# A longer look ahead before TensorE turns back from 64x64 parts, with new order and engine strings, in a fused attention and FFT-gate kernel

## The chip, the cores and the metric

One core of one Trainium2 chip. The metric is the device time of one execution in microseconds (us); lower is better. Times of the kernel before: median 951.72 us of 3 runs (948.12 to 954.63).

## The reference

For each of 8 batches, with S = 3136 rows, a model width of 256 and a key width of 64, all in float32:

```python
scores = scale * np.matmul(z, z.transpose(0, 2, 1))      # scale = 1 / S
attn = np.maximum(scores, 0.0) ** 2
x = u * np.matmul(attn, v)                               # [8, 3136, 256]

proj = x @ w_proj                                        # 256 -> 768
x1, x2, x3 = (proj[..., :D].copy(), proj[..., D:2 * D].copy(), proj[..., 2 * D:].copy())
X2 = np.fft.rfft(x2, n=S, axis=1)
H = np.fft.rfft(filter_fft, n=S, axis=0)[None, :, :]
x2_conv = np.fft.irfft(X2 * H, n=S, axis=1)
y = x1 * x2_conv * x3
return (y @ w_out).astype(np.float32)
```

The first half is attention with a squared ReLU in place of softmax, gated by u; the second a gate with a long circular convolution, done by FFT.

## The kernel before

**Tiles.** The 3136 rows of a batch are 64 x 49. They are handled as 25 tiles of 128 rows (the last has 64), and as 7 chunks of columns, `CHUNKS` = 512 five times, then 256 and 320. The matmuls are in bf16 and sum in PSUM, which is used as 4 pairs of banks (`ps_s`, 128 x 1024 float32 each). The transforms are products with matrices of sines and cosines, in two stages: the first (`dft1`, L998) over the 64, by full tables T1; the second (`forward` and `inverse`, issued by `quads`, L1100) over the 49, with tables S2 and TZ.

**Units of TensorE work.** All of TensorE's work is cut into 2637 units, each a short run of matmuls, all issued through `matmul` (L515, so all show as L516):

- S (512 units): scores of a pair of tiles for one chunk, `score_mm` (L1729), reading `zT_t`. The result is emptied from PSUM by a ReLU into R (L1919 on ACT, L1921 on DVE) and squared into A (L1928 on ACT, L1930 on DVE). The score matrix is symmetric, so part of A is also transposed by DMA into mirror tiles (`M_t`, `M2e_t`, `M2o_t`) and used for other chunks.
- w and v (648 each): the two halves of weighing v by one pair of tiles, `weigh` (L1772), reading `A_t` or a mirror tile and `v_t`. The two halves of the array's rows sum in two banks of a pair, and the halves swap banks between w and v.
- A (424): the projections (`xT_t`, `wp`) and the first stage of the transform (`x_t`, `T`). B (229) and Z (40): the filter's transform at the start, the last stage of the inverse transform (`conv_in_t`, `T`) and the output product (`wo`, `yT_t`); Z holds the late ones of the last batches.
- Q (136): the second stage of the transform, forward (`spec_in_t`, S2) and inverse (`xh`, TZ). Between the two, DVE multiplies by the filter's spectrum (L1357, L1361, L1362). Its tables are 49 or 64 rows by 64 columns.

**Forms of the array.** A Q unit runs in 64x64 parts of the array: four matmuls at a time, one for each half of the rows and of the output partitions. Any other unit runs by default in parts of 64 rows by all 128 columns, two at a time. It can also run in 64x64 parts: `parts_of` (L570) then gives two halves of the output partitions in place of one whole, and each matmul is issued as two. A few transposes at the start use the whole array. In the profile the forms are told by their shape: `64*128` or `64*64`, rows by columns.

**What sets the order.** The program is laid out ahead of time by a planner (`Plan`, `go` at L336), which walks through a string `ORDER`, one letter for a unit of TensorE; the next unit in TensorE's program is the one that the letter names. S, w and v are taken strictly in turn; A, B and Z from the first 6 of their queue and Q from the first 4, the one ready earliest. A second string, `ENGINES`, holds one letter for each of 1426 jobs that either ACT or DVE can do (the ReLU and the square, and the copies out of PSUM): a or d. The planner's own clock, with costs per operation, sets the order of the jobs on each engine. DMA queues run from SP and POOL; POOL casts u, v and z on their way in.

The form of a unit follows from the string alone:

```python
            form = "F" if task.full else "Q" if k == "Q" else "H"
            if form == "H" and self.form == "Q" and "Q" in ORDER[self.at + 1 : self.at + 1 + NEAR]:
                form = "Q"
            if self.form is not None and self.form != form:
                start += FORM
            self.form = form
```

So once a Q unit has turned the array to 64x64 parts, the units behind it stay in them as long as one of the next `NEAR` letters is a Q; otherwise they turn back. `FORM` = 0.16 us is what the planner books for a turn. `NEAR` is 6 (L44).

Of the kernel before, what the change touches and what calls it, by code (L numbers as in the profile page):

```python
# [48 lines left out]


ORDER = (
    "ASSAwSSSwvBAAvSSwSwwSvSvwvwSvvSwSvwSvSwSvwwSvwvvSwwwSwSwSvAvAwwvSSvvwAvSvSwwABvSvwvBvSwwAvwSAwSvwASA"
    "vvAvwSAwAwSvSAvAvwSAvwSwwSvAvASwwwwvvwvBBvwvSSvvwSSwBvBwvSvwSSwAvwvSvwwwAASvAwwBvBwvSwSAvvAvwSSvSwwA"
    "BASBvvwwSvwvvvSwwwSwvvSAvAvwSAvwwSAvvwAvSwwwASvvSvAwSvSwABwSBvwwSSwvwASvSvwAwvvASAvvwwSvvSASAwAwASvS"
    "wSvwBABvwAvSSwSvvwSSvwSvwwBSBvvwSwwwSvvSwAwAvSAvwAAwSvASvvAQQvAwSwwQQvAwAASvSAvAvwAwSwSwAwSAAwwASvwS"
    "vvQvvQSwvQvASvQwAwASwSAvwvASvwAvAvAwSSwwQSvAwASQvvAwQvvSAvwQSwAvwQwAwAQvASvvQvwSwwSQvAwwvSQwAvwSvQSw"
    "wSvvQwAwSAvwSwvvSvvvvSAwAwwSvvQSwAvwQSAvvSwwQASvAwwQvwvvSwQwAvASvSvwSSwAwAwSvSvvvSAwAvAwASvwSwAvAvSw"
    "wwASvSAvwvASSAvwBSwBAvvASwwSwABAwSvBBwBAwASvSvSvAwvAwvSwSwwABAABAvSvvSvSAwABvBAwAwwwSSvSvvBSvBBvwSBw"
    "AvwAwAvAvSwwwvSBSBwSvvSvAwSwABvBwAvASwSwvSAvBABSvvwwSvSwwSvAvvQAwQwwwQSwvvwQBwvQBvwQvBAvSBAvvSwAvAww"
    "ASvASvSwwwSSSwvwvwvSSvQvwQAwAQvwBwBQvvSvQvAwwwwQASvvwvBSwwvBvSwvSSvSwAvSvAQASAwQwwSSvwASAwAvSAwvQvAQ"  # L60
    "AvSvwSwwwwSSAvvAvvSwvSwwvSvSwwvASAwSvwSwvBAvBASvwSwwBSAvBAvwBSBSvwBvBAvSvAwwwwSSAvvAvSSwSwvAvABABAAv"
    "AwSwBwASBvAvBwBSvBwBwAAAvAvvSwwAvSSAvwwwSAvAvSwSvSwAwASvwvSBvBAwSAvvSwQSvwAvBQBAwwSwQwSwQvSvQwvvwQvA"
    "wAAQwAwSwBvSvSvBwvSvQvSvAwAQvBwBQwSQwwwSvwQQwSwvBvSBvAvSAvvvSAwAwSAvAwvSwvvAQAwSwwwSvvvSvSAwwSASvvBS"
    "wBSwAvASvwwwQSQvwwvvASSAvwvwSAvASwvSvwwASwAwSvvvSvAwAwSwwASAvSvBwvSwwBAvABvBvASwwASwAvABSvBSwvwvSBvS"
    "BAvAwwSwASwABvwBSAvAvSwwSwBvBABvBwwAvASwvSABvBBvABvASvwSvAwwSwASwAvSAvvSAwSAvwwSSAvAwwSQvwwQSvSvBvBA"
    "SvwABvBwvAwAQvwSvSQvwwQwSwwwAQvvvAvBQvBSwQBwwBSvSvvSAvAAwwSAvQwAQwAvwSwSAvvAwSvSvQvwQSwwBvSQvBwvSwQv"
    "vwwwSAvwSwwvvSvAvSQvwQASvwAvSwSvwASwAAwSwwSAwASASvvwwSvASwvSvAAvAwSvvAvAvwSvwSvwSvwwSBwSBwBvBSwwSvBB"
    "BBSvwwSAvAAvvSSAwvwvwSASvvvwwSAvSvAwBwBSAwwwSSwSvvAvABABAwvwASAAwASvvSwwSvSvwvvSvvSwSwAvSwvSAvSwwwBS"
    "vSwBwSvwvBBBBvSwvvwAvvwSwAAvSvwAAAwAwSAvSvAvSwAQvSwQwBvSQwwBAvAQvwvQwvAwAwQSvwSwQvBwQvwwSBvQvvSAwwQA"
    "vQvBwwSSvBvvwSwvvSwvwAASvAAwSwvQAvSwSAwwvSSvvvwQSwSvwQvwSQvSwvASAAwAwSwwQAvvSAvwvASwvAASwASvvvwwSvBS"  # L70
    "vwBwSSvvSwSAwABvBwSvSwAwBvAABvAwSwASvAAvASSwvBvBwwSwwSSvAwAvAvASwvSSvvBwBAvSwwAASwAwBAvABBvBwvSvSAvw"
    "ABvBBAwBwSAwwBSvBvSSvwwASvSAwAvAAwSvAvwSAvASvBwBAwAvSwvAwAQwwSwQSvvvSQvBvSBwwABwwSAvvBwSvQSwSwvBQvvv"
    "BQwwASAvQvQwSwwwQSvvSwQvAwvAQSvwwSvQvBwQBwSvwSwvSvAvwwAwvASAvwwSvSvQASAvvAQwSAvwSAvwASvwwwSAwAQvvSwS"
    "wSvSvwAvwvABvSwwBvSSvwAvAvwSwwSAvAAvvSAwSwSvASwABwBwBSvBwSvvSvwSwBvBSSwvvSvBwBwSAvwBAvBwASvAwwSABAvB"
    "SvSwSwAAAAvSwwvBASvABvvABwSAvBwwwSvvAvASwSvwwSSvBvSwBAwASvwwQwSQvwBvQBvwSwwQvwQwwQvwSvQwwQvSBvvBvSAv"
    "vBAvBSwwvASvSwASvwwvSSwvvwwSQvQwwwSAvSvvABwBvSvQSwwAQvSAvwQwSvQvvwAwAvBvBwSwSwwAvSvASvQwvSAvAwSwQvSv"
    "wwSwSvAwAvwwSwvASvSvwAvwwvwwZvvvvvZAAZZAABZBZZBBBZBZZBZBZBBZZZZQQQQBQBQQQQQQZZQQQQZQZZZZZZBZZZBZZZBZ"
    "BZBBBZZBBBBBZBBBBBBZZZZBBBBBBBBBBBBBB"
)

ENGINES = (
    "aadddddddadaaaddaaaaaadadadaadaaddaaaddadaaadaadadadaadddaddaaadaaaddaadaaaadaadaaadaaaadaadaadadaaa"
    "aaadadaadadaadadadadddaaaddadaaaaadaddaaaadaaaaadadaaaaaadadaaaadadaaadaaadadadaaaadaaadaaaaaaaadaad"
    "daadaadadadadaaddadaadadadaaadaaddaaaaddddaaadaaaddddaaaaaaaadaddadadaaaaaadaaddaadaaaadaaaaaaaaaada"
    "aaaddadaddaaaaaadaddaaddaddaaaaadaaadddaaaddaaaaaaaaaaaaaaaaadaaaddddaaaaddaaddadaaddaaadaaaadaaaaaa"
    "dadaadaaaadddaadadaaaadddadaaaaddadaaddadddaaaadaaadaaaaaaaddaaaaaaaaaaadaaaadaddaaaadddaaaaadaadaad"
    "aadaadaddadadadadaaaaadaaaaaaadaaaaaddadadaadaaadddadadaaadadddaaaaadaaaadaaaaadaaddaadaadaddaaadada"
    "aaaddaadadaadaadadaaaadadaaaadadadaadaaaaadaaaaddaaadddaaaaaadadaaaaadadaadaaadaddddddaaaaadaaaaaaaa"
    "daadddaadaaaaadaaddaaadaaaddaddaadaaaadaaaaaddaaaaadaaaaaddaaddadaddaaaadaadaadaddaadadadaadaaaddaaa"
    "daddaaaaaaaaaadaaaadaddaaaaaaaaaaaaaadaddddaadadadadadddaadadddddaaaaaaaadaadaaaaaadaaaadadadadaadda"  # L90
    "daaadadaaaaaadadaddaaaddaaadaaaddaaaaaaadaaaadaddaaaaddaaadaaadaaaadaaadaaddaadaaadaaadaddaadaaaaaaa"
    "adaaadaaadadaadadaaaaddadaadaadaddaddaaddaaaaaaaaaadddaaadaadadadaaddadaadaadaaadaaadaadaaaadaddadad"
    "aaadadaaaaaadaaaaddadaaddadaaadadaadaaddaaaaadadaaaaaadaaaadaaadadaadaaaadadaaadaaddddaaddaadaaaddda"
    "daaadaaadaaaaaaaaaadaaaaadaaaaadaddaadadadadaaaadaaadddaaaaadaaaaaaaaadadddaaddaaaaddaadadadadadadaa"
    "aaaaaadadaaaadaaaaaadadddaaadadaaadadaadadaddadadaaadaadadddddaaadadadaaadaadadadaadaddaaaaaaaaaaaaa"
    "aaaaaadaaaadaaaddaaadaaaaa"
)
# [1972 lines left out]
```

## Time and profile before

| | |
|---|---|
| runs | 951.72 us, 954.63 us, 948.12 us |
| the profiled execution | 950.14 us, of which the span from the first to the last instruction is 948.4 us |
| granted TensorE clock, mean | 0.997 |
| TensorE matmuls (PE) | busy 918.9 us |
| ScalarE (ACT), VectorE (DVE) | busy 833.5 us, 824.0 us |
| DMA | 170.70 MB, mean 180 GB/s |

How to read the lines of the profile below: PE is TensorE's matmuls, PEld its weight loads, which run beside them. A group of instructions has its line, engine, operation, out<-in by the program's names, the shape (for a matmul, rows*columns of the array part, then rows x streamed columns), the count, then after the bar the busy time in us and the mean length of one in ns, and after the next bar the idle time of the engine just before them and what ended it. The busy time of a group is the union of its instructions, which overlap. In a table by stage the columns are the stretch, its length and the busy time and count of PE, PEld, DVE, ACT and POOL, then the granted clock, the DMA share and GB/s. In a timeline the columns are the start, the length of the merged group, the instruction and its count. In a list of waits, the three numbers are the total in us, the number of waits and the longest.

### The profile page before, as it was taken

Reading aid. Unit: us, or ns where it says so; the run is one execution under the profiler, and the core shown is the slowest. Engines: PE = TensorE matmul, PEld = TensorE weight load, DVE = VectorE, ACT = ScalarE, POOL = GpSimd, SP = SyncE. Lnnn points to the kernel's source line nnn. Section 1 sums busy time; section 2 is a strip of 40 time slices with the busy share of each in tenths; the row PEclk is TensorE's granted clock in tenths of the full one; section 3 lists DMA queues with packets and bytes.
Section 4 is the critical chain, followed back from the end, with each engine's and each line's share of the span. In section 5 each row is a group of like instructions: output and inputs, shape, how many; then the busy total and the mean of one; then the engine's idle time right before and its main releaser. Section 6 shows DMA issues by size and latency. Waiting matters only on the chain.

```text
span 948.4 us, 30254 instructions
## 1 busy us (share of the span) xinstructions
PE 918.9 (97%) x12412; PEld 569.9 (60%) x12412; DVE 824.0 (87%) x1108; ACT 833.5 (88%) x961; POOL 238.2 (25%) x585
## 2 busy tenths in 40 slices
PE   8998999999999999999999999999999999999986
PEld 3444655666555667757565666667667666666644
DVE  8885897998778998999889998789989999899785
ACT  7977899899988997999978999889987999899573
POOL 5243322221232212223222222232123231001030
PEclk9999999999999999999999999999999999999999
DMA  9999889988999799997899989999999989996767
GB/s 153 161 177 157 133 168 178 192 138 173 164 197 199 156 169 185 214 202 166 177 188 209 178 152 192 179 188 179 165 186 215 219 146 185 198 195 157 189 185 234
DMA packets 331643, 170.70 MB, mean 180 GB/s; under 512 B 242886, under 2 KB 307142, under 8 KB 331504
## 3 DMA queue, kind: packets, MB, share of 16 engines
q1 hardware_dynamic: 301624, 131.98, 70.4%
q0 software_dynamic: 29168, 35.13, 25.9%
q8 instruction: 97, 1.59, 0.7%
q10 hardware_dynamic: 712, 1.66, 0.5%
q14 instruction: 42, 0.34, 0.1%
HBM read 90.26 MB, written 53.05 MB: 151 GB/s over the span
## 4 chain that ended last, share of the span: by engine, by line
PE 58%; DVE 7%; DMA 6%; ACT 2%; issue 2%; SPq 1%; POOL 0%; ACTq 0%; DVEq 0%; POOLq 0%
PE ps_s L516 58%; DVE xh L1357 2%; DMA M2e_t<-A_t 2%; DMA spec_in_t<-spec 1%; DVE A_t L1930 1%; DMA M_t<-A_t 1%; ACT R_t L1919 1%; ACT A_t L1928 1%; DVE xT_t L1975 1%; DMA out_dram<-ost_t 1%; DMA zn_t<-in_z_dram 1%; DMA spec<-s_t 1%; DVE yT_t L1462 1%; SPq L1062 0%; DVE R_t L1357 0%
## 5 line engine op out<-in xcount | busy, mean ns | idle before, releaser
L516 PE MATMUL ps_s<-A_t,v_t 64*128 64x512 bf16 (+5 forms) x4736 | 517.0, 353 | 0.4 <-DVE A_t L1930 0.3
L516 PEld LDWEIGHTS <-v_t 64*128 64x128 bf16 (+1 forms) x6501 | 311.5, 98 | 179.5 <-PE ps_s L516 19.2
L1919 ACT ACTIVATE R_t<-ps_s 128x1024 f32<-128x1024 f32 (+3 forms) x374 | 348.6, 960 | 38.5 <-PE ps_s L516 35.8
L1928 ACT ACTIVATE A_t<-R_t 128x1024 bf16<-128x1024 f32 (+4 forms) x268 | 261.3, 996 | 22.9 <-DMA M_t<-A_t 8.4
L1930 DVE SCALAR_TENSOR_TENSOR A_t<-R_t 128x1024 bf16<-128x1024 f32 (+2 forms) x224 | 246.2, 1115 | 19.1 <-ACT R_t L1919 13.0
L516 PE MATMUL ps_s<-zT_t 64*128 64x512 bf16 (+4 forms) x1201 | 193.3, 352 | 3.1 <-ACT R_t L1919 0.9
L1921 DVE TENSOR_SCALAR R_t<-ps_s 128x1024 f32<-128x1024 f32 (+4 forms) x138 | 153.4, 1121 | 22.4 <-PE ps_s L516 17.8
L639 POOL COPY tick<-A_t 1x1 bf16<-1x1 bf16 x159 | 44.6, 281 | 432.8 <-ACT A_t L1928 293.5
L516 PE MATMUL ps_s<-xT_t,wp 64*128 64x512 bf16 (+4 forms) x984 | 125.2, 353 | 2.7 <-ACT R_t L1919 2.4
L516 PEld LDWEIGHTS <-zT_t 64*128 64x128 bf16 (+1 forms) x1234 | 71.6, 97 | 51.0 <-issue 10.6
L516 PE MATMUL ps_s<-M_t,v_t 64*128 64x512 bf16 (+4 forms) x852 | 96.4, 354 | 0.0
L582 ACT ACTIVATE x_t<-ps_s 128x1024 bf16<-128x1024 f32 (+3 forms) x76 | 71.6, 945 | 19.8 <-PE ps_s L516 19.6
L1357 DVE TENSOR_TENSOR xh<-xh,H 128x1024 bf16<-128x1024 bf16 x120 | 82.1, 686 | 5.4 <-ACT xh L582 4.9
L1256 DVE TENSOR_TENSOR gate_t<-ps_s,x_t 128x512 bf16<-128x512 f32 (+2 forms) x112 | 64.5, 618 | 16.2 <-PE ps_s L516 12.8
L1975 DVE TENSOR_TENSOR xT_t<-ps_s,uT_t 128x512 bf16<-128x512 f32 (+2 forms) x112 | 64.0, 614 | 9.5 <-PE ps_s L516 9.2
L516 PEld LDWEIGHTS <-wp 64*128 64x128 bf16 (+1 forms) x984 | 49.2, 96 | 34.1 <-issue 4.1
L1462 DVE TENSOR_TENSOR yT_t<-ps_s,gate_t 128x1024 bf16<-128x1024 f32 (+2 forms) x53 | 57.2, 1080 | 12.2 <-PE ps_s L516 9.4
L516 PE MATMUL ps_s<-wp,xT_t 64*128 64x256 bf16 (+1 forms) x960 | 64.6, 266 | 0.2
L625 POOL DMA_DIRECT2D un_t<-in_u_dram x112 | 57.8, 517 | 20.4 <-issue 17.2
L651 POOL DMA_DIRECT2D v_t<-in_v_dram x112 | 58.1, 524 | 17.3 <-issue 13.7
L516 PE MATMUL ps_s<-wo,yT_t 64*128 64x256 bf16 (+3 forms) x888 | 60.8, 266 | 1.3 <-DVE yT_t L1462 1.1
L516 PEld LDWEIGHTS <-xT_t 64*128 64x128 bf16 (+1 forms) x960 | 45.1, 97 | 15.8 <-issue 0.7
(158 smaller groups left out, 904.3 us busy)
## 6 DMA issues: line engine op xcount, KB each, us to landing
out_dram<-ost_t SPq DMA_DIRECT2D x60, 256.0 KB
spec_in_t<-spec SPq DMA_DIRECT2D x56, 192.0 KB
spec<-gs_t SPq DMA_DIRECT2D x56, 192.0 KB
v_t<-in_v_dram POOLq DMA_DIRECT2D x80, 128.0 KB, 4.5
un_t<-in_u_dram POOLq DMA_DIRECT2D x80, 128.0 KB, 4.5
spec<-s_t SPq DMA_DIRECT2D x40, 256.0 KB
...
```

The costliest lines, as they stand in the source:

```text
L516: got = nc.tensor.matmul(o, *args, **kw)
L582: got = nc.scalar.activation(out_, in_, AF.Copy)
L625: nc.gpsimd.dma_start(out=t[ds(j * N1, N1), lo - t0 : hi - t0, :], in_=x[:, n2 : n2 + hi - lo, :])
L651: nc.gpsimd.dma_start(out=t[ds(j * N1, N1), ds(v_at(a), (b - a) * D)], in_=r[:, n2 + a - lo : n2 + b - lo, :].rearrange("p t d -> p (t d)"),)
L1256: has_read(nc.vector.tensor_tensor(o[:, :, ::-1] if h == 0 else o, p, x, ALU.mult), p)
L1357: nc.vector.tensor_tensor(x[:, 1 - i], x[:, 0], h, ALU.mult)
L1462: has_read(nc.vector.tensor_tensor(yb["y"][:, :, 0:w], p, gates[b, c][:, :, 0:w], ALU.mult), p)
L1919: has_read(nc.scalar.activation(r, p, AF.Relu), p)
L1921: has_read(nc.vector.tensor_single_scalar(r, p, 0.0, ALU.max), p)
L1928: nc.scalar.activation(a, r, AF.Square, scale=1.0 / float(S))
L1930: nc.vector.scalar_tensor_tensor(a, r, inv_s2, r, ALU.mult, ALU.mult)
L1975: has_read(nc.vector.tensor_tensor(x[:, :, ::-1] if h == 0 else x, f, ut, ALU.mult), f)
```

## The change

`NEAR` becomes 24, and the strings `ORDER` and `ENGINES` are replaced by new ones of the same length and with the same number of each letter of the order. No matmul, copy, DMA or buffer is added or removed as a piece of work; units in 64x64 parts are issued as twice as many matmuls of half the output partitions. The diff, with most lines of the strings left out (the lines of the order shown are letters 400 to 499):

```diff
-NEAR = 6
+NEAR = 24
...
 ORDER = (
...
-    "vvQvvQSwvQvASvQwAwASwSAvwvASvwAvAvAwSSwwQSvAwASQvvAwQvvSAvwQSwAvwQwAwAQvASvvQvwSwwSQvAwwvSQwAvwSvQSw"
...
+    "vSvvwSvwSQwAvAAQvAwQSwvSvASAvvAwAwSvSwvQvAQwSwAvAvSAwwASwAQvQwvwAQvAQwwSvQvvwSvSwwSvwSQvvSwAQwAwvSvv"
...
 ENGINES = (
-    "aadddddddadaaaddaaaaaadadadaadaaddaaaddadaaadaadadadaadddaddaaadaaaddaadaaaadaadaaadaaaadaadaadadaaa"
...
+    "aadddddddaadaaadaadaaaaadadadaaaddaadadaaaadadadadaddadaadaadaadaadaaddaddaaaaadaaaaddaaaadaaddddaaa"
...
```

Of the 2637 places of `ORDER`, 718 hold the same letter in both; of the 1426 of `ENGINES`, 565 differ, and d (DVE) stands 500 times in place of 479.

More of the change, by code (lines that the diff above doesn't have):

```diff
@@ L57 @@
[L57 to L61, printed above, removed]
@@ new lines @@
+    "vASAvSwwSvSwwvSvAvvSvvwwAwwSASvAwSSvwSvBvABvASwvBSvBSwwSwBwABvBAvBSwvSvSvwwAwAASvSAwSvvwASAAvAwABvAS"
+    "wBvwBSwBvSAwABwBBwBAvvAAvSAvvwSwAwAASvwSvAwvSvSBvSwBvASwAwwSAvSwAQSvwvwSSvQvvABwAwQwBvQwSvwSvQSwwQwv"
+    "QAvAwwSSvvQwBvBvASASwvQvvAwABwBQvvSwSwwBSvQvBwvSQwwQvvAwwSAAvAvSAvAwwSvvwSwQvwSvwwSvwvSvAASAAwBvBQwv"
+    "wSvvSwAwASvQwwSwASvwSASwvvSvwvSAvSwASwwAwAvSvSvvAvAwwSwwASAvwSSBvBvAwAvSBwSBvSvSwvBwBAwSAvvAwABAvBAS"
+    "vwAvwwBAwBSvSwwvBvSBvvSAwABwBASvAwASvAwSBvBBwSBwvSwASvAvvSwwAvSAvwASvASwwASvASwvAwASSvwwSQAvAwBSBvQw"
@@ new lines @@
+    "vSBwvBSvwwvvQwvSAvAwwQASvAwSwwQwwQBwBBvBQwAvASvvQvvSvSwvSwAwAQAvAvwSQvSwwSAvSvvwAQvwwSQvwQwwvSSvvvwS"
+    "BwBvvwQSwwwQvvvAwSSvAAwSAvQvwSSAvwSAwSvwAvSwAASAvAwSwwSwSwvASvAvvAwvSvwSvwAvASvwwSvwSBwvBSvvSBwBSwBw"
+    "BSvvwSvAwABvwSwvSBvvASwAAvAwwSAvAvwwBSSvBwwAvSAvSvwSSwvSAwAvwwSBSwvBvAvSAwvwBwAwBSAvvvvSwSwwwvSBwSBB"
+    "vBvAwSAvSwSwvSSvvwvwAvAASwAwSQwvASwABvABvAvQvSwSAwSAvSvwwQvQvAwAQvwASvAwwwwQSvSwwQvBvvBSQvvwQSwwwQAv"
+    "SvASvwwBSvBvvSwwwSvvQwwAvSAQvvwASAvSwwQwSSvvvwAwSAvQwwSwvSwAAAAvwSvvSwQSwvQvwSwSAvAvAvASwvAvASwSwBwS"
@@ new lines @@
+    "BvSvwBAvASwvBwSBvSBwSvwSAvwAAwAvSvASvAwSwASvAvwwSwSvAwAwBABAvSvBSvBwSwwASvAAAvvBwSvBBvSwBwAwSAvvABAv"
+    "ABAwSwSwBwSwSwBBvBvSvvSwAvSvAwSwABAAwwABAvASvSwvSvAQAwvwSvvwSwvASwQAwwBvSBBwvBvSQvQwSvwAASAwwSAQvvvQ"
+    "vvwQvwSBwBSvQvwSQwwASvAQwvvQSvwBwwQBvvvSSwwwwvvSvQvwwwSAwAvwSSvvQvwAQAvASvASwAvSAAwASvAwAwSAwwwAvSSw"
+    "vvSwSwASwAvvSQvvwAvAwvSvSvwwSwSvAwASvAvSASwvBSwwBwSSvBwBSvwwvBvBSBvBvSvBwSBvwwASwASvwAvvABAwBAvSwSAv"
+    "ABwBBABAwSwwBAvASBvvSSvAwSvwSAvvBwwSBwSwwAwwSASvvvSvSSvwSwBvBwQQwwSvAvAwvQvvwvSwwSwQwQQvvvvQBvBSwvBw"
@@ L79 @@
+    "SSBvvwwQSvAvAwwAvSvwAwwSvSwQSwwSwvAQvBAvvBSSvQwwQvSAwAvQSvwvwSAvAvBwwBQvwvwAvvSSwAvwSwvwQSAvAwvQvwSw"
+    "wSSvvAvSwASvwwSAvvAwSSvwwZvvwwwvvvZZAAZAABZBZBZBBZBBBZZZZBBZZZZQQQQQQQQQQQQZBQQQQZBBZBZZZZZZBZZBZZZZ"
+    "ZBBBZBZBBBBBZBBZBBBZZZZBBBBBBBBBBBBBB"
 )
 ENGINES = (
[L82 to L84 removed]
@@ new lines @@
+    "adaaaaaaaadaddadadaadadaaaadaaaadddaaaadaaaaadddadaaadaaaaaaaadaadaaaaaaaddadaaaaaaadddaaaaaaddadaad"
+    "adaadaadadadadaaaaadaaaaaddaadaaaaaadadaaaaaaaadddaadadaadaddaaaadadadaaaadaadaaadadddadaddaaaaaaaaa"
+    "daddaaadddaaddaaadaaadaaddaaadaaaddaaaaaaaaaaaadadaaddadadadadadaaddaaddaaadaaaaaddaadaaaaaddaaaaaaa"
+    "aaddadaaaaaaddaddadaaaadaaadaaadaaaddaaaaadaaaadaaadadadadadaaddaaaaadaaaaadaddddadadadaaaaaaddaaaad"
+    "adddadaadadadadaaddaaadaaaaaaadaadaaaaadaaaadadaaaddaaddaadaaaaddaddaaddaaadaaaaddaadaaadddaaddaaadd"
@@ L97 @@
+    "adaaadadadaaaaaddaddaaaaad"
 )
```

49 lines of the change are left out of this document (16 added, 33 removed).

## The prediction

> **What bounds the kernel now.** I read the page first (busy shares, granted clock, the chain that ended last), then the busy times by stage, then single stretches of the TensorE timeline. The page:
>
> ```profile
> span 948.4 us, 30254 instructions
> PE 918.9 (97%) x12412; PEld 569.9 (60%) x12412; DVE 824.0 (87%) x1108; ACT 833.5 (88%) x961; POOL 238.2 (25%) x585
> PEclk9999999999999999999999999999999999999999
> PE 58%; DVE 7%; DMA 6%; ACT 2%; issue 2%; SPq 1%; POOL 0%; ACTq 0%; DVEq 0%; POOLq 0%
> ```
>
> TensorE is busy for 97% of the span at full clock and holds 58% of the chain; the two engines that empty PSUM have about an eighth of the span free. By stage (columns: stretch, its length, then busy time and instructions of each engine):
>
> ```profile
> 0.00:25.00 25.00, 21.43 (x144) 8.28 (x144) 21.26 (x55) 18.29 (x25) 13.18 (x35) 1.00 1.09 151
> 25.00:150.00 125.00, 122.41 (x1305) 65.73 (x1305) 100.09 (x130) 108.22 (x125) 37.95 (x90) 0.99 1.03 163
> 150.00:275.00 125.00, 122.75 (x1763) 75.00 (x1761) 110.37 (x140) 115.63 (x129) 33.08 (x83) 1.00 0.98 169
> 275.00:400.00 125.00, 121.02 (x1697) 81.22 (x1692) 108.78 (x143) 112.02 (x127) 31.20 (x80) 1.00 1.03 185
> 400.00:525.00 125.00, 123.60 (x1680) 75.97 (x1677) 113.31 (x152) 112.88 (x129) 30.06 (x74) 1.00 0.99 190
> 525.00:650.00 125.00, 123.81 (x1710) 78.17 (x1708) 109.68 (x144) 115.62 (x129) 33.73 (x84) 1.00 1.03 183
> 650.00:775.00 125.00, 124.65 (x1797) 84.92 (x1794) 115.52 (x156) 116.18 (x134) 33.66 (x82) 1.00 0.99 182
> 775.00:900.00 125.00, 123.93 (x1726) 78.56 (x1724) 109.43 (x143) 109.36 (x126) 13.87 (x37) 1.00 0.87 183
> 900.00:948.40 48.40, 35.31 (x620) 22.08 (x615) 35.54 (x54) 25.30 (x45) 11.49 (x22) 0.98 0.73 209
> ```
>
> Between 25 and 900 us TensorE is without a matmul for 875.0 - 862.2 = 12.8 us; before that for 3.6, after it for 13.1. So a new order of the same matmuls can win at most some 13 us in the middle from visible waits, plus what is lost in steps too short to show as idle. The turns between the two array forms are such steps.
>
> **The turns.** This stretch has both directions, and the same kinds of unit in both forms (start, length of the merged group, then the instruction and its count):
>
> ```profile
> 202.86 0.38 PE L516 MATMUL ps_s<-M2o_t,v_t 64*128 64x256 bf16 x4
> 203.08 0.38 PE L516 MATMUL ps_s<-M_t,v_t 64*128 64x256 bf16 x4
> 203.39 0.41 PE L516 MATMUL ps_s<-spec_in_t,S 49*64 49x512 bf16 x4
> 203.63 0.31 PE L516 MATMUL ps_s<-zT_t 64*64 64x320 bf16 x4
> 203.77 0.60 PE L516 MATMUL ps_s<-A_t,v_t 64*64 64x256 bf16 x16
> 204.21 0.60 PE L516 MATMUL ps_s<-xT_t,wp 64*64 64x512 bf16 x8
> 204.64 0.39 PE L516 MATMUL ps_s<-M_t,v_t 64*64 64x256 bf16 x8
> 204.86 0.39 PE L516 MATMUL ps_s<-A_t,v_t 64*64 64x256 bf16 x8
> 205.08 0.39 PE L516 MATMUL ps_s<-xh,TZ 64*64 64x512 bf16 x4
> 205.39 0.31 PE L516 MATMUL ps_s<-zT_t 64*128 64x320 bf16 x2
> 205.54 0.59 PE L516 MATMUL ps_s<-xT_t,wp 64*128 64x512 bf16 x4
> 205.97 0.27 PE L516 MATMUL ps_s<-A_t,v_t 64*128 64x256 bf16 x2
> ...
> 876.69 0.41 PE L516 MATMUL ps_s<-xh,TZ 64*64 64x512 bf16 x4
> 877.03 0.83 PE L516 MATMUL ps_s<-A_t,v_t 64*128 64x256 bf16 x12
> ```
>
> Starts are to be read, not lengths, since a matmul's length contains the pipeline's own depth. Four 64*128 matmuls of 256 columns step 0.22 us (202.86 to 203.08); the same four take 0.31 when a 64x64 group follows (203.08 to 203.39): a turn into 64x64 costs 0.09. A 64x64 group of 512 columns steps 0.215; followed by a 64*128 one it takes 0.31 (205.08 to 205.39) or 0.34 (876.69 to 877.03): a turn back costs 0.09 to 0.13. Over all turns of the trace I take the middle, 0.107 us.
>
> **The change, part by part.** (1) How many turns. The rule is a function of the order string alone, so I stepped it through both strings. Before, with 6 units looked ahead, there are 64 turns, and 367 units that are not of the second stage run in 64x64 parts. After, with 24, there are 18 turns in 9 stretches (one long stretch a batch, 118 to 204 units, one of a single unit, and the tail), and 910 such units. So 46 turns go: 46 x 0.107 = **-4.9 us**, between 46 x 0.09 = -4.1 and 46 x 0.13 = -6.0. No other engine hides them: they lie on TensorE, which is the bound there. All but the tail's lie between 25 and 900 us.
>
> (2) What the 543 more units in 64x64 parts cost. Each is issued as twice as many matmuls and weight loads. The same projection unit takes 0.43 us as eight 64*64 matmuls (204.21 to 204.64) and 0.43 us as four 64*128 ones (205.54 to 205.97); the weighing by 256 columns takes 0.22 us in both (204.64 to 204.86; 202.86 to 203.08). Grouped:
>
> ```profile
> L516 PE MATMUL ps_s<-A_t,v_t 64*128 64x512 bf16 x2342 | 333.2, 378 | 0.1
> L516 PEld LDWEIGHTS <-v_t 64*128 64x128 bf16 x4543 | 242.6, 94 | 154.6 <-PE ps_s L516 18.0 <-issue 9.8 <-DMA M_t<-spec_in_t 0.5
> L516 PE MATMUL ps_s<-A_t,v_t 64*64 64x512 bf16 x1172 | 88.1, 376 | 0.0
> L516 PEld LDWEIGHTS <-v_t 64*64 64x64 bf16 x1958 | 69.0, 106 | 24.9 <-PE ps_s L516 1.2 <-issue 0.7
> ```
>
> Per unit of work that is 333.2/2342 = 0.142 against 2 x 88.1/1172 = 0.150, 5.7% more, but these are unions of lengths, in which waits at the edges of short stretches count. So the bounds are 0 by the timeline and, by the groups, 543 units x 918.9/2637 us each (TensorE's busy time over the string's 2637 units) x 5.7% = +10.8. I take 0, because the steps are the more direct reading; what hides the doubled loads is the stream of columns: they run beside it. If that cover were gone, it is the +10.8.
>
> The rule that speaks against: by the Trainium skill's TensorEngine Tiling (Array Packing), Restrictions and Gotchas, column tiling does without the fast weight load, so four loads of 64 columns would stand beside each group. As an estimate by the time of a load in TensorE: Matmul & The Clock Gate of the Trainium skill, LDWEIGHTS (columns over 1.2 per ns), 4 x 53 = 213 ns would outlast a 256-column group if they queued. The trace disagrees: sixteen 64*64 matmuls of 256 columns, four groups, step 0.44 us (203.77 to 204.21), 0.11 a group, though a load there is 106 ns long. The same tiling page says that a switch of mode drains the array, and the 0.09 to 0.13 agrees.
>
> (3) The moved units. Both strings are new: only 718 of 2637 places of the order hold the same letter, and 565 of the 1426 choices of engine differ. Of TensorE's work nothing is added or removed, so the streaming sum stays; what can move is the 12.8 us of visible waits and the small ones. S, w and v are taken strictly in turn, so the lead of each weighing over the scoring that feeds it can be stepped through the string with the stream times above. Leads under 3 us: 8 of 648 before, 15 after; what they lack to 3 us sums to 6.9 before, 10.0 after. That is slightly tighter, +3.1 at most from this source. On the other side nothing shows which of the other waits go; the unknown runs from -12.8 (all visible waits in the middle gone) to +17.8 (worked out below). I take 0: the tightening is nearer to nothing than either end.
>
> (4) The engine string. ACT's share falls from 947 to 926 jobs, DVE's rises from 479 to 500. Nearly all are one pass over a pair of banks:
>
> ```profile
> L1919 ACT ACTIVATE R_t<-ps_s 128x1024 f32<-128x1024 f32 x302 | 302.0, 1028 | 33.2 <-PE ps_s L516 31.3 <-ACT S L880 0.4
> L1921 DVE TENSOR_SCALAR R_t<-ps_s 128x1024 f32<-128x1024 f32 x106 | 128.2, 1219 | 14.7 <-PE ps_s L516 12.6 <-ACT A_t L1928 0.6 <-ACT R_t L1919 0.2
> ```
>
> ACT loses 21 x 1.028 = 21.6 (833.5 to about 812), DVE gains 21 x 1.219 = 25.6 (824.0 to about 850, 90% of the span). That lies beside TensorE's work and costs nothing while the engine that is later still has slack; DVE becomes the fuller one. By the string's order 10 of the moved jobs are in the first eighth of the choices and 13 in the second, where DVE has the most room (100.1 and 110.4 of 125).
>
> **The sum.** The profiled execution took 950.14 us, 1.6 under the runs' median of 951.72 (948.12 to 954.63). 950.14 - 4.9 + 0 + 0 = 945.2; on the median's footing 951.72 - 4.9 = **946.8**, which I predict. That is 0.5%, less than the 1% that a measurement of this kernel can surely tell from no change.
>
> **The rivals.**
>
> *The new order also sheds waits.* For it: they are few and single, so another order can miss them; the longest on TensorE are
>
> ```profile
> PE ps_s L516 <- ACT xh L582: 3.5, 3, 1.4
> PE ps_s L516 <- ACT R_t L1919: 3.3, 3, 2.4
> PE ps_s L516 <- DVE tick L678: 1.7, 1, 1.7
> ```
>
> Against it: the leads are no longer. Half of the 12.8 and 3 of the 13.1 in the tail: 946.8 - 6.4 - 3.0 = 937.4.
>
> *DVE takes over as the bound (slower).* The place is the first two batches, 23 more passes on DVE. The fullest that DVE gets in any stage is 115.5 of 125, 92.4%. In 150 to 275 us it would hold 110.4 + 13 x 1.219 = 126.3; at 92.4% that needs 136.7 us, 11.7 more than the stage has; if half of the 10 passes of the first batch also come late, 6.1 more: 946.8 + 17.8 = 964.6. It decides from about 92% DVE busy over a stage. For it: units of the second stage have DVE passes of their own in the same stretches. Against it: the batches straddle the stages, and ACT is relieved by as many jobs.
>
> *The gain is given back by tighter leads.* 46 turns saved, 3.1 us of lead lost: 949.9.
>
> *64x64 parts are dearer after all.* The groups' 5.7%: 946.8 + 10.8 = 957.6. Against it, the equal steps.
>
> That the change doesn't do what it says can be excluded as to the count of turns, which follows from the string.
>
> **How the numbers follow.** Forecast 0.50, waits shed 0.22, DVE 0.12, given back 0.11, dearer parts 0.05. Faster by over 1% (under 942.2): the 0.22 and 0.03 from the forecast's lower edge, 0.25. Slower by over 1% (over 961.2): the 0.12 and 0.01 of the dearer parts, 0.13. Within 1%: 0.62. The forecast's own range, with the runs' spread of 3 each way and the turns' bounds, is 941 to 953. The range over all cases has to take in the shed waits (937.4 less 3) and the dearer parts (957.6 and 2), and stops short of most of the DVE case: 934 to 960.
>
> **What would show it.** Right: about 18 steps of 0.09 to 0.13 where the form turns, about eight long runs of 64*64 groups in which 512 columns still step 0.215 us, TensorE busy about 914 us, idle between 25 and 900 us still 8 to 18 us, ACT near 812, DVE near 850. The first term is wrong if the turns stay many or were hidden in waits; the second if 64*64 groups step longer than 0.215; the third and fourth if idle time of TensorE behind DVE's passes is over 20 us in the middle, most likely between 25 and 275 us.

## The result, and the profile after

The changed kernel takes 962.45 us (median of 20 runs, 952.35 to 971.13), the kernel before beside it on the same chip 951.59 us (20 runs, 946.64 to 957.99). The ratio is 1.0091, with a 95% interval of 1.0066 to 1.0117: slower by 0.9%, where 946.8 us was forecast, and outside the range. Two more measurements of it in later sets (new_24_again and new_24_third below) gave 1.0193 (1.0119 to 1.0268) and 1.0127 (1.0076 to 1.0178). The profiled execution took 958.07 us (span 956.3), 4.4 under the median of its kernel; that of before took 950.14 (948.4). The profile of old_all64 below is of a slow execution (981.51 us), so of it only counts and the stalls of one kind are read.

The page of after, with the instruction queue of DMA, which the prediction did not look at (the columns of a queue are packets, MB, share of the 16 engines' span):

```profile
span 956.3 us, 34645 instructions
PE 914.9 (96%) x14609; PEld 588.5 (62%) x14609; DVE 845.7 (88%) x1130; ACT 814.7 (85%) x939; POOL 250.7 (26%) x585
q8 instruction: 114, 1.87, 0.8%
```

The same queue in the page of before:

```profile
q8 instruction: 97, 1.59, 0.7%
```

TensorE is busy 4.0 us less (918.9 to 914.9), close to the 4.9 that the turns were to save (the mean granted clock is 0.990 in place of 0.997, so that the two are not quite comparable). ACT and DVE are at 815 and 846, near the 812 and 850 worked out, and yet the span is 7.9 us longer. TensorE's program has 2197 more matmuls, and so many more weight loads, in 17 more packets of instructions. By stage (the columns as in the prediction):

```profile
0.00:25.00 25.00, 20.57 (x150) 8.69 (x152) 21.68 (x55) 18.75 (x26) 13.22 (x35) 0.93 1.12 150
25.00:150.00 125.00, 115.61 (x1245) 62.42 (x1245) 102.18 (x136) 97.26 (x107) 38.19 (x86) 0.97 1.04 152
150.00:275.00 125.00, 124.14 (x2140) 80.61 (x2130) 113.58 (x143) 114.51 (x128) 38.05 (x83) 1.00 1.05 176
275.00:400.00 125.00, 119.77 (x1920) 74.46 (x1919) 111.84 (x143) 104.19 (x119) 31.41 (x77) 0.99 1.05 176
400.00:525.00 125.00, 122.94 (x2151) 79.86 (x2147) 114.66 (x150) 112.25 (x126) 35.00 (x81) 1.00 1.07 190
525.00:650.00 125.00, 122.65 (x2021) 78.87 (x2014) 113.24 (x148) 111.20 (x127) 33.65 (x82) 1.00 1.06 182
650.00:775.00 125.00, 122.18 (x2160) 86.42 (x2155) 112.70 (x153) 113.48 (x130) 29.95 (x77) 1.00 0.99 185
775.00:900.00 125.00, 124.59 (x2135) 90.55 (x2126) 112.58 (x147) 114.63 (x136) 18.92 (x43) 1.00 0.94 178
900.00:956.30 56.30, 42.45 (x735) 26.61 (x735) 43.21 (x63) 28.45 (x47) 12.27 (x23) 0.96 0.76 220
```

Between 25 and 900 us TensorE is idle for 875.0 - 851.9 = 23.1 us in place of 12.8. Of that, 9.4 lie in the stage of 25 to 150 us (2.6 before) and 13.7 in 150 to 900 us (10.2 before). The first is nearly one stall, here in the timeline and in the waits of TensorE and DVE:

```profile
77.02 1.21 PE L516 MATMUL ps_s<-M2e_t,v_t 64*128 64x512 bf16 x8
84.76 0.61 PE L516 MATMUL ps_s<-zT_t 64*128 64x512 bf16 x2 [6.52 <-DVE xT_t L1975]
```

```profile
PE ps_s L516 <- DVE xT_t L1975: 7.5, 2, 6.5
PE ps_s L516 <- ACT R_t L1919: 3.4, 4, 1.6
PE ps_s L516 <- DMA spec_in_t<-spec: 2.6, 3, 1.0
PE ps_s L516 <- DVE yT_t L1462: 2.4, 5, 1.0
PE ps_s L516 <- DMA M_t<-A_t: 2.3, 2, 1.4
```

```profile
DVE zd_t L1613 <- DMA zn_t<-in_z_dram: 8.9, 2, 8.1
```

The copy of z on DVE waits 8.1 us for its DMA, the operation on xT_t starts right behind it, and TensorE waits for that one. With the stall the granted clock falls: to half for 6.8 us from 81.3 us on (0.97 in the stage). At 77 us no unit of the second stage has run on TensorE yet and the array is in 64*128 parts, so this stall is no matter of the look ahead. It is one of the new strings: a repeat of the kernel with these strings and 6 letters has it too (experiment 1), without much loss. What makes the rest slower is the question of the experiments. One thing is settled by the timeline already, the steps of the long 64*64 runs:

```profile
204.87 0.66 PE L516 MATMUL ps_s<-A_t,v_t 64*64 64x512 bf16 x8
205.31 0.66 PE L516 MATMUL ps_s<-xT_t,wp 64*64 64x512 bf16 x8
205.74 0.45 PE L516 MATMUL ps_s<-M2o_t,v_t 64*64 64x256 bf16 x8
205.96 0.45 PE L516 MATMUL ps_s<-M_t,v_t 64*64 64x256 bf16 x8
206.17 0.66 PE L516 MATMUL ps_s<-xT_t,wp 64*64 64x512 bf16 x8
```

Eight matmuls of 512 columns still step 0.43 to 0.44 us (204.87 to 205.31 to 205.74) and eight of 256 step 0.22, as before. The loss is not in the steps.

### The profile page after: what moved, and what is told of

It is laid out like the page before. It is cut to its first block, busy times and chain, and to the rows that moved or that the text cites. A ratio compares the mean times of both kernels' runs of the same rounds, so it can differ in the third digit from the quotient of the medians.

```text
span 956.3 us, 34645 instructions
## 1 busy us (share of the span) xinstructions
PE 914.9 (96%) x14609; PEld 588.5 (62%) x14609; DVE 845.7 (88%) x1130; ACT 814.7 (85%) x939; POOL 250.7 (26%) x585
## 4 chain that ended last, share of the span: by engine, by line
PE 51%; DMA 6%; DVE 4%; ACT 3%; issue 2%; SPq 1%; ACTq 0%; DVEq 0%
PE ps_s L516 51%; DMA M_t<-A_t 2%; ACT R_t L1919 1%; DVE A_t L1930 1%; DMA M2e_t<-A_t 1%; DMA M2o_t<-A_t 1%; DMA uT_t<-un_t 1%; DVE xh L1357 1%; DMA conv_in_t<-spec 1%; DVE yT_t L1462 1%; DVE xh L586 1%; DMA spec_in_t<-spec 1%; SPq L1848 0%; ACT A_t L1928 0%; DVE gs_t L586 0%
## 5 line engine op out<-in xcount | busy, mean ns | idle before, releaser
L516 PE MATMUL ps_s<-A_t,v_t 64*64 64x512 bf16 (+5 forms) x5660 | 519.4, 350 | 1.4 <-issue 0.8
L516 PEld LDWEIGHTS <-v_t 64*64 64x64 bf16 (+1 forms) x7866 | 326.2, 102 | 173.6 <-PE ps_s L516 20.1
L1928 ACT ACTIVATE A_t<-R_t 128x1024 bf16<-128x1024 f32 (+2 forms) x281 | 272.9, 995 | 21.9 <-DMA M_t<-A_t 10.2
L1930 DVE SCALAR_TENSOR_TENSOR A_t<-R_t 128x1024 bf16<-128x1024 f32 (+4 forms) x211 | 231.6, 1117 | 15.9 <-ACT R_t L1919 7.7
L516 PE MATMUL ps_s<-zT_t 64*128 64x512 bf16 (+4 forms) x1452 | 196.1, 348 | 11.6 <-DVE xT_t L1975 7.5
L1921 DVE TENSOR_SCALAR R_t<-ps_s 128x1024 f32<-128x1024 f32 (+2 forms) x153 | 171.9, 1134 | 25.4 <-PE ps_s L516 22.1
L516 PE MATMUL ps_s<-xT_t,wp 64*64 64x512 bf16 (+4 forms) x1128 | 125.7, 355 | 0.2
L516 PEld LDWEIGHTS <-zT_t 64*64 64x64 bf16 (+1 forms) x1485 | 74.0, 101 | 58.8 <-issue 19.5
L516 PE MATMUL ps_s<-M_t,v_t 64*64 64x512 bf16 (+5 forms) x1048 | 98.6, 348 | 4.1 <-DMA M_t<-A_t 2.3
L1256 DVE TENSOR_TENSOR gate_t<-ps_s,x_t 128x512 bf16<-128x512 f32 (+2 forms) x112 | 64.5, 618 | 10.8 <-PE ps_s L516 7.1
L516 PEld LDWEIGHTS <-wp 64*128 64x128 bf16 (+1 forms) x1128 | 50.0, 99 | 27.5 <-PE ps_s L516 2.3
L516 PE MATMUL ps_s<-wp,xT_t 64*64 64x256 bf16 (+3 forms) x1176 | 65.5, 266 | 0.2
L516 PE MATMUL ps_s<-wo,yT_t 64*128 64x256 bf16 (+1 forms) x968 | 61.3, 265 | 2.2 <-DVE yT_t L1462 2.0
L651 POOL DMA_DIRECT2D v_t<-in_v_dram x112 | 58.6, 527 | 18.0 <-issue 12.8
```

Source lines behind the costliest of these rows:

```text
L516: got = nc.tensor.matmul(o, *args, **kw)
L651: nc.gpsimd.dma_start(out=t[ds(j * N1, N1), ds(v_at(a), (b - a) * D)], in_=r[:, n2 + a - lo : n2 + b - lo, :].rearrange("p t d -> p (t d)"),)
L1256: has_read(nc.vector.tensor_tensor(o[:, :, ::-1] if h == 0 else o, p, x, ALU.mult), p)
L1921: has_read(nc.vector.tensor_single_scalar(r, p, 0.0, ALU.max), p)
L1928: nc.scalar.activation(a, r, AF.Square, scale=1.0 / float(S))
L1930: nc.vector.scalar_tensor_tensor(a, r, inv_s2, r, ALU.mult, ALU.mult)
```

## The experiments

The strings and the looking ahead come from one search, but they can be taken apart: the planner's schedule is left as it is in the kernel named, and only the form in which a unit is issued is decided again, with its own number of letters:

```diff
+SHOWN = 24
...
+            shown = "F" if task.full else "Q" if k == "Q" else "H"
+            if shown == "H" and self.shown == "Q" and "Q" in ORDER[self.at + 1 : self.at + 1 + SHOWN]:
+                shown = "Q"
+            self.shown = shown
...
-        return [slice(0, N1), slice(N1, P)] if plan.form == "Q" else [slice(0, P)]
+        return [slice(0, N1), slice(N1, P)] if plan.shown == "Q" else [slice(0, P)]
```

"old" and "new" name the strings, the number is `SHOWN`, "all64" is 4000 letters. Order, engines, DMAs and buffers are those of the strings. The added lines move `matmul` from L516 to L521 and further, so its line number differs from run to run. The theories at the start: the new strings place the work worse (T1); the 64x64 parts cost something that the steps don't show (T2).

### 1. Strings and forms apart

**old_24.** 

> The old strings and the old schedule of every engine; only the form in which a unit is issued follows the rule with 24 units looked ahead. 36 turns in place of 64, 228 more units in 64x64 parts. If 64x64 parts are free and a turn costs 0.107 us: 28 turns less, -3.0 us, about 948.6. If 64x64 parts are dearer by the groups' 5.7%, 0.020 us a unit: -3.0 + 4.5, about 953.

**old_all64.** 

> The old strings and schedule; from the first unit of the second stage to the last, every unit is issued in 64x64 parts: 2 turns in place of 64, 1722 more units in 64x64 parts. If 64x64 parts are free: 62 x 0.107 = -6.6 us, about 945. If they are dearer by 0.020 us a unit: +34.3 - 6.6, about 979. If the doubled instructions are fetched or issued too slowly, TensorE shows new idle time that ends in nothing.

**new_6.** 

> The new strings and the schedule of the changed kernel; only the form in which a unit is issued follows the rule with 6. 132 turns in place of 18, 722 fewer units in 64x64 parts. If the loss of the changed kernel comes from where the new strings put the units, and turns cost 0.107 us: +12.2 us over the changed kernel, about 974. If the loss came from 64x64 parts: 12.2 - 14.4, about 960, no slower than the changed kernel.

**new_all64.** 

> The new strings and schedule; every unit between the first and the last of the second stage is issued in 64x64 parts: 2 turns in place of 18, 1179 more units in 64x64 parts. If the strings' places for the units are the cause: -1.7 us from the changed kernel, about 960, and still about 15 us over the old strings in the same form. If 64x64 parts are the cause: +23.5 - 1.7, about 984.

| kernel | turns | other units in 64x64 parts | us (range) | ratio to before (95%) |
|---|---|---|---|---|
| before | 64 | 367 | 951.86 | |
| old_24 | 36 | 595 | 952.21 (946.23 to 961.37) | 1.0011 (0.9973 to 1.0049) |
| old_all64 | 2 | 2089 | 969.79 (961.88 to 981.51) | 1.0172 (1.0115 to 1.0229) |
| new_6 | 132 | 188 | 952.79 (947.7 to 956.3) | 1.0019 (0.9989 to 1.0049) |
| after | 18 | 910 | 962.45 | 1.0091 (1.0066 to 1.0117) |
| new_all64 | 2 | 2085 | 967.26 (961.55 to 977.27) | 1.0156 (1.0099 to 1.0213) |

T1 falls: with the forms of 6 letters the new strings are as fast as the old within 0.5%, DVE at 846 us busy in both new_6 and after. T2 stands: with the new strings and their schedule untouched, forms by 24 letters in place of 6 lose 962.45 - 952.79 = 9.7 us though they save 114 turns, and with the old strings all64 loses 17.9 us though it saves 62. So of the change's loss the strings with 6 letters make 952.79 - 951.86 = 0.9 us, and the look ahead nearly all the rest. The step to old_24 (+0.35 us) is not clear of noise. As to the times expected, new_6 came out under both (974 and 960), and new_all64 between its two (960 and 984). The loss is also not the same for each unit: from 24 letters to all64 the new strings turn 1175 more units to 64x64 parts, and the medians differ by only 4.8 us (967.26 - 962.45). A later repeat of new_6 gave 1.0053 (1.0023 to 1.0083); its profile holds the stall on z and xT_t as well, 6.2 us long, in a span of 949.2:

```profile
PE ps_s L521 <- DVE xT_t L1980: 7.9, 3, 6.2
```

### 2. What is it in the 64x64 parts

The traces of the two all64 kernels hold what that of before has not at all and that of after only twice: stalls of TensorE that no semaphore ends ("issue"). In after, new_all64 and old_all64, in this order:

```profile
PE ps_s L516 <- issue: 1.1, 2, 0.8
```

```profile
PE ps_s L521 <- issue: 6.5, 7, 2.1
...
q8 instruction: 151, 2.47, 1.1%
```

```profile
PE ps_s L521 <- issue: 7.5, 9, 1.9
...
q8 instruction: 151, 2.47, 1.1%
```

One of them closely, in the timeline of new_all64, and the instruction queue between 576.3 and 577.5 us of it:

```profile
577.14 0.41 PE L521 MATMUL ps_s<-xT_t,wp 64*64 64x256 bf16 x6
578.70 0.30 PE L521 MATMUL ps_s<-xT_t,wp 64*64 64x256 bf16 x2 [1.14 <-issue]
578.70 0.83 PE L521 MATMUL ps_s<-A_t,v_t 64*64 64x320 bf16 x16
```

```profile
q8 instruction: 1, 0.02, 5.8%
```

TensorE stops in the middle of a unit, after six of its eight matmuls. The queue's packet (16 KB; 19,326 matmuls and as many loads in 151 packets are 256 instructions each) runs from 576.33 to 577.44 us, 8.8 us after the one before it began, where the median between two packets of this kernel is 5.8. TensorE goes on 1.26 us after the packet's end. The other stalls over 0.6 us of this kind start again 1.42 to 1.48 us after the end of a packet, the six of old_all64 1.36 to 1.62. So there the program itself arrives late. In all these stalls are 6.5 and 7.5 us, less than half of what the two kernels lose, and in after 1.1 us. In before the median between packets is 9.2 us, in after 7.5.

The theory that follows (T2a): issued in 64x64 parts, the same work needs twice the instructions; their packets must pass DMA engines that are busy all the time (the DMA share in the table by stage is about 1), and TensorE stops when one is late. Its rival (T2b): the 64x64 matmuls or loads cost on TensorE itself. Four kernels on one chip; the first part of the diff is that of old_split, the second that of the light ones:

```diff
     def matmul(o, *args, **kw):
+        if plan.col is not None:
+            w, x = args
+            i = plan.col
+            o, x = (y[:, i * (y.shape[1] // 2) : (i + 1) * (y.shape[1] // 2)] for y in (o, x))
...
-                    if j in only:
+                    if j in only and b >= B - 2:
```

**old_split.** 

> The old strings, schedule and forms, with 64 turns; but each unit that the run with every unit in 64x64 parts had turned to 64x64 is issued here in parts of 64x128 as twice as many matmuls of half the columns. The number of TensorE instructions is that of the run in 64x64 parts (some 14,000 more than before), the form is the old one. Each of some 3,500 additional pairs of matmuls costs the 2.4 ns that a step has over its columns, +8.5 us. If the loss of 64x64 parts (24 us in 1722 units, once the 62 turns are counted) comes from the form of the array: 952 + 8.5, about 960. If it comes from the doubled instructions: 952 + 8.5 + 24, about 985, with stops of TensorE that no semaphore ends.

**old_0.** 

> The old strings and schedule; only units of the second stage run in 64x64 parts, and the array turns back behind each: 244 turns in place of 64, 367 fewer units in 64x64 parts, some 3000 TensorE instructions fewer. By 0.107 us a turn and nothing for a unit: +19.3, about 971. By 0.107 a turn and 0.014 us a unit as the old strings showed: +19.3 - 5.2, about 966. If a turn is mostly hidden: under 960.

**light_6.** 

> The kernel before without the output stores of the first six batches (their outputs stay unwritten), some 19 MB of 171 MB of DMA less. If the waits of the kernel before are of late transfers, 3 to 8 us less than before, about 946; else 952.

**light_all64.** 

> The old strings with every unit between the first and the last of the second stage in 64x64 parts, and without the output stores of the first six batches. If 64x64 parts lose because more instructions have to be fetched past full DMA engines, the loss against the same kernel with all its stores shrinks when transfers are fewer: 955 or less, under 12 us over the light kernel in the old form. If they lose in the array or at issue, it stays at 18 us over it.

| kernel (before beside them: 951.08) | matmuls in its program | us (range) | ratio to before (95%) |
|---|---|---|---|
| old_split | 19,493 | 970.07 (965.09 to 978.96) | 1.0215 (1.0161 to 1.0268) |
| old_0 | 10,927 | 957.56 (951.57 to 960.86) | 1.0081 (1.0051 to 1.011) |
| light_6 | 12,412 | 940.81 (937.22 to 945.24) | 0.9903 (0.9872 to 0.9934) |
| light_all64 | 19,319 | 951.52 (944.65 to 957.23) | 1.0015 (0.9982 to 1.0049) |

old_split never leaves 64x128 for the units in question and is as slow as old_all64: twice the instructions without the 64x64 form lose as well. But the time lies between the two expected ones, 960 if it were the form and 985 if it were the instructions, so it decides for neither alone. Its trace has the stalls and the packets too:

```profile
PE ps_s L533 <- issue: 3.7, 5, 1.4
...
q8 instruction: 152, 2.49, 1.1%
```

Some of its loss is its own: a step of n columns takes about n/2.4 + 2.4 ns in the traces (56, 109 and 216 ns at 128, 256 and 512 columns), and 3,540 more pairs of matmuls make 8.5 us. Some 10.5 of its 19.0 us over before are left for the instructions, where all64 loses 17.9 with 62 turns saved. With 19 MB of stores less the old kernel itself falls by 10.3 us, more than the 3 to 8 expected, and the loss of all64 falls from 17.9 us (969.79 - 951.86) to 10.7 (951.52 - 940.81). So part of the loss depends on how full the DMA is. That is what T2a says, but data that come late through the DMA would do the same; and all64 keeps stalls on issue even there:

```profile
PE ps_s L521 <- issue: 4.1, 4, 1.7
...
q8 instruction: 151, 2.47, 1.1%
```

old_0 gives the price of a turn: 180 turns more and 367 units fewer in 64x64 parts cost 957.56 - 951.08 = 6.5 us. A line through before, old_24, old_all64 and old_0 gives 0.059 us a turn and 0.0127 us a unit in 64x64 parts, each known to about a third: two turns saved pay for 2 x 0.059 / 0.0127 = 9 units. Looking 6 letters ahead is under that, looking 24 ahead over it. By these prices the change would be worth -46 x 0.059 + 543 x 0.0127 = +4.2 us, less than half of the 10.9 measured.

### 3. The look ahead of 24 itself

**old_marks** adds, in the old strings, only instructions:

```diff
+            if self.seen and "Q" in ORDER[self.at + 1 :]:
+                self.blank(NOPS)
...
+    def blank(n):
+        for _ in range(n):
+            nc.tensor.sem_inc(spare_sem)
```

> The kernel before with its own strings and forms (64 turns, 367 units in 64x64 parts), and from the first second-stage unit to the last six extra instructions in TensorE's program per unit, each only adding one to a spare semaphore that nobody waits for: about 13,300 more instructions, as many as the kernel with all units in 64x64 parts has, and not one more matmul, weight load or turn. If it is the fetching of the longer program that costs, about 18 us more than before as there (965 to 972), about 150 packets on the instruction queue, and stalls of TensorE that end some 1.3 to 1.6 us after such a packet. If it is the doubled matmuls and weight loads themselves, not over 954. If the extra instructions hold up TensorE's sequencer by themselves, steps between matmuls grow everywhere, also where no packet is near, and the time is well over 972.

It took 2253.91 us (2252.79 to 2257.46), ratio 2.3776. It is the third case: the added instructions hold up TensorE by themselves, (2253.91 - 949.21) us / 13,344 = 98 ns each, at a mean clock that is lower as well (0.707). It says nothing on the packets.

**new_light_6.** 

> New strings, forms by 6 letters looked ahead (132 turns, 188 other units in 64x64 parts), and the output of the first six batches is computed but not written to memory (it is left out), some 19 MB of DMA less. The old strings fell from 951 to 940.8 by that; as the new ones with forms by 6 stood 1.8 us above the old, both theories expect 941 to 944.

**new_light_24.** 

> The changed kernel with the output of the first six batches computed but not written (left out). Against the same with forms by 6: with full DMA the step from 6 to 24 cost 9 to 10 us. If the loss is instruction packets that wait behind full DMA engines, it shrinks, to 2 to 6 us (943 to 949). If the 64x64 parts cost on TensorE itself, or the long stretches collide with ACT or DVE, it stays at 9 to 10 (951 to 954).

**new_24_again.** 

> The changed kernel's forms once more, beside the three others on one chip: 958 to 963 by its first measurement. By the prices taken from the old strings (0.059 us a turn, 0.0127 us a unit in 64x64 parts), 46 turns less and 543 units more give +4.2 us against before, 955 to 956; a time nearer to that says that the first measurement also held some luck, one of 960 and more that the longer stretches cost more in the new order than in the old.

Measured on one chip (before 949.21 us): new_light_6 945.89 (944.57 to 950.88), new_light_24 945.18 (942.7 to 951.89), new_24_again 966.34 (961.73 to 975.68), so the first measurement of after was no bad luck. new_light_6 fell less than expected (941 to 944): by 6.9 us from new_6, where the old strings fell by 10.3. With the lighter DMA the loss from 6 to 24 letters is gone: -0.7 us, where it was 9.7 between their first measurements (962.45 - 952.79). So the loss of the changed kernel is not a cost of the same 14,609 matmuls in the same forms on TensorE alone (T2b). A smaller cost there is not excluded: 114 turns saved should have won 6.7 us at 0.059 each, and won 0.7. The rows for the stretch from 150 to 900 us (busy time and instructions of PE, PEld, DVE, ACT, POOL, then clock, DMA share, GB/s) of new_24_again, new_6, new_light_24 and new_light_6, in this order:

```profile
150.00:900.00 750.00, 733.87 (x12457) 492.61 (x12448) 675.97 (x875) 668.82 (x759) 186.93 (x441) 1.00 1.02 181
```

```profile
150.00:900.00 750.00, 742.81 (x9620) 443.54 (x9618) 680.28 (x880) 671.52 (x761) 188.17 (x441) 1.00 1.01 182
```

```profile
150.00:900.00 750.00, 743.08 (x12594) 497.29 (x12584) 684.14 (x886) 672.16 (x764) 190.62 (x445) 1.00 0.93 159
```

```profile
150.00:900.00 750.00, 748.97 (x9740) 446.06 (x9737) 686.83 (x888) 674.83 (x765) 190.99 (x445) 1.00 0.91 158
```

The idle time of TensorE is 750 less the busy one: 16.1 and 7.2 us with the DMA at a share of 1.01 to 1.02, 6.9 and 1.0 with it at 0.91 to 0.93. 24 letters add 9 us of waits on the full DMA and 6 on the light one, where they are no more than the turns saved (the profile of new_light_24 is of an execution of 950.1 us, 4.9 over its median, so the 6 are rather too many). So there is a second candidate beside T2a (T2c): with fewer turns TensorE is earlier at data that come late through the DMA, and the gain ends in waits. The half clock behind long waits adds little: the mean clock of the runs is 0.991 in new_6 and 0.990 to 0.991 in the three measurements of the changed kernel, some 1 us. The last kernels were to tell these two apart; new_split keeps the 132 turns but has just the changed kernel's number of instructions:

```diff
+FAR = 24
...
+            far = "F" if task.full else "Q" if k == "Q" else "H"
+            if far == "H" and self.far == "Q" and "Q" in ORDER[self.at + 1 : self.at + 1 + FAR]:
+                far = "Q"
+            self.far = far
+            self.halved = shown == "H" and far == "Q"
```

**new_split.** 

> New strings with the forms of 6 letters (132 turns); each unit that 24 letters would put in 64x64 parts stays in 64x128 and is issued as twice as many matmuls of half the columns, so that TensorE's program is exactly as long as the changed kernel's (14,609 matmuls) and no turn is saved. Twice as many matmuls cost something by themselves: in the old strings some 8.5 us for 1722 units, so 3.6 us for these 722. If the length of the program is what costs under full DMA: 952.8 + 3.6 + the 10 to 13 us that 24 letters lost, 966 to 970. If it is that fewer turns bring TensorE to late data: 952.8 + 3.6, 955 to 958.

**new_light_split.** 

> The same with the output of the first six batches computed but not written (left out). Forms by 6 took 945.9 there. If the length of the program costs only under full DMA: 945.9 + 3.6 + 0 to 4, 949 to 953. If twice as many matmuls cost on TensorE itself far more than 3.6 us, it stays as far above 945.9 as new_split is above 952.8.

**new_12.** 

> New strings, forms by 12 letters: 72 turns, 468 other units in 64x64 parts, 12,810 matmuls. Between 6 letters (11,706 matmuls, 952.8) and 24 (14,609, 962 to 966). By the prices of a turn and a unit from the old strings the same as 6 letters, 952 to 954; by a line through the measured ends 956 to 958.

**new_24_third.** 

> The changed kernel's forms beside the three others on one chip, so that its distance to new_split is taken there: 961 to 967 by its two measurements before.

And two of them once more, side by side on another chip:

**new_split_again.** 

> The same kernel as in the run before (the length of the changed kernel's program, 132 turns). Against new_6 on the same chip: 13 us and more above it if the length of the program is the whole of the loss, 2 to 5 us if it is late data alone, 6 to 10 if it is about half.

**new_6_again.** 

> New strings, forms by 6 letters: 0 to 3 us above before, as measured.

| kernel | us (range) | ratio to before (95%) |
|---|---|---|
| new_split | 959.69 (958.5 to 968.08) | 1.0118 (1.0062 to 1.0174) |
| new_light_split | 951.87 (948.96 to 958.08) | 1.0046 (1.0013 to 1.0078) |
| new_12 | 957.0 (952.51 to 966.48) | 1.0096 (1.0062 to 1.0131) |
| new_24_third | 962.79 (958.65 to 967.37) | 1.0127 (1.0076 to 1.0178) |
| new_split_again | 964.0 (960.8 to 969.44) | 1.0174 (1.014 to 1.0208) |
| new_6_again | 953.38 (948.48 to 960.45) | 1.0053 (1.0023 to 1.0083) |

new_split is 10.6 us above new_6 on one chip (964.0 - 953.38), on the light DMA 6.0 (951.87 - 945.89). Both of its times with full DMA lie between those expected for one theory and for the other. The 6.0 are the doubled matmuls themselves, more than the 3.6 expected; TensorE's busy time says the same, in new_light_split and new_light_6:

```profile
PE 923.8 (97%) x14609; PEld 624.9 (66%) x14609; DVE 846.7 (89%) x1130; ACT 816.8 (86%) x939; POOL 252.7 (27%) x585
```

```profile
PE 918.3 (97%) x11706; PEld 538.2 (57%) x11706; DVE 845.1 (90%) x1130; ACT 815.9 (86%) x939; POOL 252.5 (27%) x585
```

That is 5.5 us more. What is left, 10.6 - 6.0 = 4.6 us, would be what a longer program costs at full DMA without a turn saved, as T2a says. But each of these differences is known only to some 5 us (the intervals of the ratios, added up), so the 4.6 are not clear of nothing, and 9.7 + 0.7 us hang on full DMA in the changed kernel. Nor do the traces show them as waits. The rows of new_split and new_split_again:

```profile
150.00:900.00 750.00, 743.53 (x12411) 528.03 (x12409) 676.23 (x873) 670.14 (x758) 187.28 (x441) 1.00 1.01 180
```

```profile
150.00:900.00 750.00, 740.01 (x12403) 526.54 (x12395) 675.91 (x871) 668.52 (x755) 186.79 (x441) 1.00 1.00 179
```

With as many instructions as the changed kernel, but 132 turns, TensorE is idle for 6.5 and 10.0 us there, where new_6 and new_6_again have 7.2 and 6.2 and the three profiles of the changed kernel 13.7, 16.1 and 20.2. The idle time goes with the turns saved more than with the length of the program, which speaks for T2c in the changed kernel; that the longer program has a share is possible and not shown. new_12 (957.0) came out where a line through 6 and 24 letters has it, and over the 952 to 954 of the old strings' prices, as both theories allow. In new_24_third the idle time of 150 to 900 us is the largest of the changed kernel's three, and its longest entries behind the stall on xT_t (6.6 us) are data, while stalls on issue make 1.1 us:

```profile
PE ps_s L521 <- ACT R_t L1924: 5.3, 7, 1.8
PE ps_s L521 <- DMA M_t<-A_t: 4.4, 2, 3.6
PE ps_s L521 <- DMA spec_in_t<-spec: 3.2, 4, 1.4
```

In the trace of after itself, five waits between 300 and 540 us (0.35 to 0.89 us each, 3.4 together) end 1.25 to 1.54 us after a packet, the delay of the stalls on issue, though three of the five name data; the rest of its 13.7 us are waits for data. In new_24_again the waits that end so make 1.0 of 16.1 us. Left open: whether a late packet also starts the later waits for data, and why waits at late data should cost more than the turns had saved. No trace here shows when a packet was asked for.

No version tried is faster than the kernel before with the whole output stored: forms by 6 letters have the lowest median in both strings, in the old ones level with 24.

## Why the prediction was wrong, step by step

**The failed step is (2), that the 543 more units in 64x64 parts cost nothing** because "what hides the doubled loads is the stream of columns". The steps are equal, as read, so the sign that was to show this step wrong, steps over 0.215 us, never came. The runs show the cost all the same: 722 more units in 64x64 parts, with nothing else changed but 114 turns saved, lose 9.7 us in the new strings, and with 19 MB less of DMA nothing (-0.7 us). The step was priced on the engine alone, while the DMA share of about 1 stood in the same profile, and the cost depends on it. In the old strings such a unit costs 0.0127 us, 6.9 us for 543; in the new ones, from 6 to 24 letters, more ((9.7 + 114 x 0.059) / 722 = 0.023). By which way the full DMA makes the cost stays open: late instructions are seen, but only as 1.1 us of stalls on issue in the changed kernel, and waits for data hold most of its added idle time. The upper bound of +10.8 from the groups' lengths equals the loss of 10.9 by luck: those lengths hold pipeline and waits, and no loss of steps. That rival (957.6, chance 0.05) was told as longer steps, which it is not.

**Step (1), the turns**, is right in kind, and its term is too large. That the turns fall from 64 to 18 holds, and those read closely are steps of 0.09 to 0.13 longer; TensorE's busy time fell by 4.0 us against 4.9, at a lower clock. But a turn is worth 0.059 us of time, by the line through the old strings, not 0.107. On TensorE alone it is no more: old_0 is busy for 930.1 us with 180 turns more, 11.2 us over before or 0.062 a turn, so the 0.107, read at three places, did not hold for turns in general. There is something of the rival "given back" (949.9) too: idle time between 150 and 900 us rose from 10.2 to 13.7 in the profile of after, to 16.1 and 20.2 in two others. It named tighter leads as its cause; that the light DMA cuts the waits points at late data.

**Step (3), the moved units at 0**, holds for the sum: new_6 is 0.2 and 0.5% above before, with 68 turns more and 179 fewer units in 64x64 parts. It hid two parts: a stall of 6.5 us near 80 us that the old order had not, and fewer waits later (7.2 us in new_6 between 150 and 900 us against 10.2). The idle time between 25 and 900 us, 23.1, lies outside the 8 to 18 that were named as a sign of being right, and 6.5 of it are that stall.

**Step (4), the engine string at 0**, holds: ACT 814.7 and DVE 845.7 against about 812 and 850 expected, and new_6 carries the same load at no loss. DVE as the new bound (964.6) has nearly the measured time and is not the cause.

**The rule weighed under (2)**, that of the Trainium skill's TensorEngine Tiling (Array Packing), Restrictions and Gotchas, on loads without the fast path, would have given a loss too. The steps of 0.11 us a group at 256 columns say in after, as they did before, that it is not what costs here. Of instruction fetch the Trainium skill says, in Runtime: NRT & Kernel Launch, Instruction fetch mechanics, that crossing to the next block is mostly hidden. Before agrees, with no stall on issue, and so nearly does after, with 1.1 us; the all64 kernels, with 6.5 and 7.5 us of them at full DMA, do not.

**The range** was too narrow upwards because all of the unknown costs were taken on TensorE, ACT and DVE, and none on the full DMA, which feeds TensorE with data and with instructions.
